# Linear attention beside a gated FFN on one core: exp and phi over two banks, rstd for two tiles, K's banks in turns, and the query projection of twelve tiles moved in front of gate/up

## The chip, the core and the metric

The kernel runs on one core of one Trainium2 chip. The metric is the device time of the whole program in microseconds. The kernel before takes 510.51 us (median of 4 runs, 510.33 to 510.68).

The core has five engines that run side by side, each with its own queue that is worked strictly in order: PE (TensorE, matrix products), DVE (VectorE), ACT (ScalarE), POOL (GpSimd) and SP (SyncE, which here only issues transfers). They wait for each other through semaphores. PE writes its results into PSUM, eight banks of 512 fp32 values in each of 128 partitions; DVE and ACT read them from there.

## The reference

The input x has 2048 tokens of width 576. It is normalised once, and two branches are added to it: a linear attention with 32 heads of width 18, and a gated FFN of width 4608.

```
xn   = (x - mean) / sqrt(var + 1e-5)
q, k, v = xn @ wqkv                       # 32 heads of 18
phi(t)  = where(t > 0, t + 1, exp(t)) + 1e-6
kv   = sum over tokens of phi(k) v^T      # per head, 18 x 18
z    = sum over tokens of phi(k)
o    = phi(q) kv / (phi(q) z + 1e-6)
out  = x + o @ wo + (gelu(xn @ w_gate) * (xn @ w_up)) @ w_down
```

All tensors are bf16; sums are taken in fp32.

## The kernel before, in words

The 2048 tokens are 16 tiles of 128. The program has a head and then four chunks of four tiles each.

**The head** works tile by tile. For tile n: `ln_half` (two statistics over column halves of 288, DVE), `ln_aggr` (DVE), `ln_rstd` (two ACT instructions, a logarithm and an exponential), the normalisation `xn` (on DVE for even tiles, on ACT for odd tiles from 3 on, the latter after a small POOL instruction `ln_bias`), and its transpose `xnT`, for tiles 0 and 1 on PE with copies by ACT and DVE, from tile 2 on by a DMA that SP issues. Then PE projects K (and for some tiles Q): `kq_mm`, five matmuls of 288 columns for each half of the columns, each half in a bank of its own. Q uses banks 6 and 7, K uses banks 4 and 5 (`KQ_BANK`). For each half, `kq_exp` (ACT) takes the exponential of k - 1 out of PSUM, and `kq_phi` (DVE) forms max(min(e, 1), k), again from PSUM; the constants that this leaves off are put back elsewhere. The next projection into a bank waits until `kq_phi` has read it. `g_accumulate` (PE, seven matmuls for a tile) sums xn^T phi(k) over the tiles in banks 0 to 3, so that K's values need not be kept and V is never projected: kv follows later from this sum and V's weights (`kv_part`). `z_add` (POOL) sums phi(k) over the tiles.

In what follows K5 is the ten matmuls of tile 5's K, Q2 those of tile 2's Q, G4 the seven matmuls of `g_accumulate` for tile 4, and xnT7 the DMA transpose of tile 7.

**The order in the head is written out by hand.** Every piece is a `step` with a name, and the string `HEAD` lists the names in the order in which they are issued: s statistics, a aggr, r rstd, b bias, n norm, t PE transpose, c the copy or DMA transpose, m a half of a projection (tile, 1 for K and 0 for Q, half), e exp, p phi, z, G, x the load of a tile, w some idle matmuls, B and g small POOL work. What the string leaves out is added in the order that a small planning function finds. As each engine's queue is in order, the string fixes each queue. The seconds written in the `step` calls serve the planner alone.

**Q of the other tiles** is projected later. `LATE` names them: 5, 6, 7, 9, 10, 11, 12, 13, 14, 15. `late_q` runs them at the start of the chunk that holds the tile. There PE works as two row tiles of 64 rows, side by side (`_Unit`): 18 matmuls of 64 rows and 288 columns for each tile, two at a time, and ACT and DVE form phi from them in `_LateQ.end`.

**After the head** the sum is copied out of PSUM (`g_copy`, `g_strip`), multiplied with V's weights and masked. Then each chunk runs late Q, 18 gate/up pairs (`gu_pair`, PE with gelu on ACT and the product on DVE, weights streamed from HBM into four rotating buffers), and the down projection of its four tiles with the attention output added (`_DownTile`). In each chunk the DVE forms the denominators of the chunk's four tiles between the gate/up pairs (`den_jobs`), from phi(q).

SP's queue issues the transfers in order: the loads of x, the DMA transposes, V's weights, the first four weight blocks of gate/up.

Of the kernel before, what the change touches and what calls it, by code (L numbers as in the profile page):

```python
# [8 lines left out]
ACT = mybir.ActivationFunctionType  # L9
ALU = mybir.AluOpType  # L10
BF16 = mybir.dt.bfloat16
F32 = mybir.dt.float32
# [3 lines left out]
P = 128  # L16
HP = 64
S = 2048
D = 576
# [3 lines left out]
NS = S // P  # L23
# [4 lines left out]
HALF = D // 2  # L28
# [14 lines left out]
Q_CUT = 3  # L43
LATE = (5,6,7,9,10,11,12,13,14,15)
PK0 = 4
# [15 lines left out]
def kernel(  # L61
# [171 lines left out]

    def ln_rstd(n):
        r = rstd[:, n:n + 1]
        nc.scalar.activation(out=r, in_=mv[:, n, 1:2], func=ACT.Ln, bias=eps_ln[:], scale=1.0)
        nc.scalar.activation(out=r, in_=r, func=ACT.Exp, scale=-0.5)

    def ln_bias(n):
        nc.gpsimd.tensor_scalar(  # L240
            out=nbias[:, n:n + 1], in0=mv[:, n, 0:1], scalar1=rstd[:, n:n + 1], scalar2=-1.0, op0=ALU.mult, op1=ALU.mult,
        )
# [36 lines left out]

    KQ_BANK = (6, 4)  # L280
    e_tiles = {}

    def kq_mm(n, which, hf):
        c = which * D + hf * HALF
        for kt in range(KT):
            nc.tensor.matmul(  # L286
                ps_all[:, KQ_BANK[which] + hf, :HALF], lhsT=xnT[:, kt, n * P:(n + 1) * P],
                rhs=wqkv_sb[:, kt, c:c + HALF], start=(kt == 0), stop=(kt == KT - 1),
            )

    def q_first(k0, k1):
        for kt in range(k0, k1):
            for hf in range(2):
                nc.tensor.matmul(  # L294
                    ps_all[:, KQ_BANK[0] + hf, :HALF], lhsT=xnT[:, kt, 0:P], rhs=wqkv_sb[:, kt, hf * HALF:(hf + 1) * HALF],
                    start=(kt == 0), stop=(kt == KT - 1),
                )

    def kq_exp(n, which, hf):
        e = e_tiles[n, which, hf] = awork.tile([P, HALF], F32, name="phi_e", tag="phi_e", bufs=8)  # L300
        nc.scalar.activation(  # L301
            out=e[:], in_=ps_all[:, KQ_BANK[which] + hf, :HALF], func=ACT.Exp, bias=neg1[:], scale=1.0,
        )

    def kq_phi(n, which, hf):
        nc.vector.scalar_tensor_tensor(  # L306
            out=(pq, pk)[which][:, n, PK0 * which + hf * HALF:PK0 * which + (hf + 1) * HALF], in0=e_tiles[n, which, hf][:], scalar=1.0,
            in1=ps_all[:, KQ_BANK[which] + hf, :HALF], op0=ALU.min, op1=ALU.max,
        )

# [149 lines left out]
    def step(name, *args, **kw):  # L462
        steps[name] = _Step(*args, **kw)
# [7 lines left out]
    W_AT = {1: 5.60, 0: (7.65, 8.45)}  # L471

    for n in range(8, NS):
        step(("x", n), "SP", 0.58, n / 2 - 2, [], lambda n=n: load_x(n, 1), ready=9.70, tail=2.6)
    for n in range(NS):
# [5 lines left out]
        step(("aggr", n), "DVE", 0.14, n - 2.1 + lead, [("stats", n, 0), ("stats", n, 1)], lambda n=n: ln_aggr(n), tail=0.07)  # L481
        step(("rstd", n), "ACT", 0.43, n - 2.1 + lead, [("aggr", n)], lambda n=n: ln_rstd(n), tail=0.07)
        if n < TD:
            for i, (k0, k1, eng) in enumerate([(0, 3, "ACT"), (3, KT, COPY[n])]):
                b = TP_BANK[n] - i
                if NORM[n] == "A":
                    if not i:
                        step(("bias", n), "POOL", 0.20, n - 2.1 + lead, [("rstd", n)], lambda n=n: ln_bias(n))
                    step(("norm", n, i), "ACT", (0.49, 0.36)[i], n - 2.1 + lead, [("bias", n)],
                         lambda n=n, k0=k0, k1=k1: ln_norm_act(n, k0 * P, min(k1 * P, D)))  # L490
                else:
                    step(("norm", n, i), "DVE", (0.26, 0.19)[i], n - 2.1 + lead, [("rstd", n)],
                         lambda n=n, k0=k0, k1=k1: ln_norm(n, k0 * P, min(k1 * P, D)), tail=0.05)
# [5 lines left out]
        else:  # L499
            if NORM[n] == "P":  # L500
                step(("norm", n), "POOL", 2.35, n - 2.1 - GL, [("rstd", n)], lambda n=n: ln_norm_pool(n))
            elif NORM[n] == "A":
                step(("bias", n), "POOL", 0.15, n - 2.1, [("rstd", n)], lambda n=n: ln_bias(n))
                step(("norm", n), "ACT", 0.77, n - 2.1, [("bias", n)], lambda n=n: ln_norm_act(n), tail=0.09)
            else:
                quiet = [("z", m) for m in range(1, n) if Z_BEHIND[m] < n][-1:]
                step(("norm", n), "DVE", 0.36, n - 2.1, [("rstd", n)] + quiet, lambda n=n: ln_norm(n), tail=0.07)
            step(("xnT", n), "SP", 1.25, n - 1.9, [("norm", n)], lambda n=n: dma_transposes(n), tail=1.6)
            ready = [("xnT", n)]
        for which, rank in ((1, n), (0, n + 0.6))[:1 if n in LATE else 2]:  # L510
            for h in range(2):
                r = rank + h / 100
                last = [m for m in range(n) if which or m not in LATE][-1:]
                free = [("phi", m, which, h) for m in last]
                if n == which == 0:
                    k0, k1 = ((0, Q_CUT), (Q_CUT, KT))[h]
                    step(("mm", 0, 0, h), "PE", 0.246 * (k1 - k0), r, ready + [("mm", 0, 0, 0)][:h],
                         lambda k0=k0, k1=k1: q_first(k0, k1), ready=W_AT[0][h], tail=0.15)
                else:
                    step(("mm", n, which, h), "PE", 0.615, r, ready + free + [("spin",)], lambda n=n, w=which, h=h: kq_mm(n, w, h),  # L520
                         ready=W_AT[which] if which else W_AT[0][1], tail=0.15)
                step(("exp", n, which, h), "ACT", 0.46, r + 0.10, [("mm", n, which, 1 if n == which == 0 else h)],
                     lambda n=n, w=which, h=h: kq_exp(n, w, h), tail=0.03)
                step(("phi", n, which, h), "DVE", 0.37, r + 0.15, [("exp", n, which, h)],
                     lambda n=n, w=which, h=h: kq_phi(n, w, h), tail=0.08)
        if n > 0:
            idle = [("norm", Z_BEHIND[n])]
            step(("z", n), "POOL", 1.40, n + 2.0, [("phi", m, 1, h) for m in (0, n) for h in range(2)] + idle + ([("z", n - 1)] if n > 1 else []),
                 lambda n=n: z_add(n, Z_BEHIND[n]))
        clear = [] if n else [("xnT", m, i) for m in range(TD) for i in range(2)]  # L530
        step(("G", n), "PE", 0.75, n + 1.15, [("phi", n, 1, 0), ("phi", n, 1, 1)] + clear, lambda n=n: g_accumulate(n, G_A))
    step(("spin",), "PE", 0.30, -1.0, [("tp", 0, 1)], lambda: spin(5))
# [4 lines left out]
    def in_order(steps):  # L537
# [17 lines left out]
    HEAD = """  # L555
        s0.1 s0.0 a0 r0 s1.1 n0.0 n0.1 s1.0 t0.0 a1 t0.1 w c0.1 c0.0 s2.1 r1 m0.1.1 e0.1.1 s2.0 m0.1.0 n1.1 a2 n1.0
        t1.1 r2 m0.0.0 p0.1.1 t1.0 m0.0.1 n2 s3.1 e0.1.0 c1.1 c1.0 e0.0.1 m1.1.1 e0.0.0 p0.1.0 s3.0 a3 p0.0.1 s4.1
        s5.0 r3 m1.1.0 m1.0.1 p0.0.0 G0 e1.1.1 m1.0.0 s4.0 e1.1.0 b3 p1.1.0 p1.1.1 c2 x9 a4 n3 m2.1.0 x8 m2.1.1
        e1.0.1 r4 e1.0.0 s5.1 B p1.0.1 e2.1.1 a5 n4 p1.0.0 e2.1.0 G1 r5 b5 p2.1.1 s7.0 m2.0.1 c3 x10 m2.0.0 p2.1.0
        s6.1 e2.0.1 n5 p2.0.1 c4 m3.1.1 m3.1.0 s6.0 e3.1.1 s7.1 e3.1.0 m3.0.1 p3.1.1 e2.0.0 a6 p3.1.0 a7 r6 r7 s8.1  # L560
        n6 G2 m4.1.1 m4.1.0 e4.1.1 s8.0 G3 p4.1.1 b7 a8 e4.1.0 p4.1.0 c5 p2.0.0 x11 c6 z1 n7 m5.1.1 x13 s9.1 s9.0 z2
        e5.1.1 m5.1.0 p5.1.1 e5.1.0 r8 a9 m3.0.0 r9 p5.1.0 c7 e3.0.1 G4 b9 m6.1.1 s10.0 e3.0.0 s10.1 n8 e6.1.1
        p3.0.1 x12 m6.1.0 G5 s13.0 m4.0.1 p6.1.1 e6.1.0 a10 p6.1.0 c8 m7.1.1 x14 m7.1.0 s11.0 n9 p3.0.0 s11.1 r10 z3
        e7.1.1 e7.1.0 e4.0.1 s12.1 a11 m4.0.0 p7.1.0 p7.1.1 z4 G6 r11 m8.1.0 n10 c9 m8.1.1 e4.0.0 e8.1.0 G7 x15
        s12.0 e8.1.1 p4.0.1 b11 p8.1.0 p8.1.1 z5 m9.1.0 n11 a12 c10 e9.1.0 s13.1 s14.1 z6 m9.1.1 p9.1.0 e9.1.1 G8
        r12 a13 r13 p9.1.1 m10.1.0 b13 m10.1.1 s14.0 e10.1.0 n12 c11 e10.1.1 G9 a14 c12 z7 p10.1.0 p10.1.1 n13
        m11.1.0 m11.1.1 p4.0.0 m8.0.1 s15.0 m8.0.0 e11.1.0 z8 s15.1 p11.1.0 r14 m12.1.0 e11.1.1 e8.0.1 a15 p11.1.1
        m12.1.1 r15 e12.1.0 c13 b15 G11 n14 p12.1.0 z9 z10 e12.1.1 m13.1.0 p12.1.1 m13.1.1 g n15 e13.1.0 c14 p8.0.1
        p13.1.0 G10 e13.1.1 c15 p13.1.1 m14.1.0 m14.1.1 e8.0.0 z11 e14.1.0 e14.1.1 G13 z12 p14.1.0 m15.1.0 e15.1.0
        p14.1.1 p8.0.0 m15.1.1 G14 z13 z14 G12 e15.1.1  # L570
    """
# [316 lines left out]
```

## Time and profile before

The profiled execution took 510.54 us by the device's count, with a span from its first to its last instruction of 508.8 us; 1.7 us lie around the span. The granted TensorE clock was 1.00 throughout.

| stretch | us from the span's start | what PE does |
|---|---|---|
| start | 0 to 9.5 | idle matmuls, then tile 0's transposes and projections as data arrive |
| head | 9.5 to 43.9 | K, Q and G of tiles 1 to 15 |
| end of the head | 43.9 to 53.9 | the rest of G, V's weights |
| chunk 0 | 53.9 to 165 | gate/up, down |
| chunks 1 to 3 | 165 to 508.8 | late Q, gate/up, down |

| group | count | mean ns |
|---|---|---|
| K and Q projections, 128 x 288 (L286) | 210 | 286 |
| rstd, logarithm (L236) and exponential (L237), one column | 16 each | 288 and 203 |
| statistics of a half (L229) | 32 | 446 |
| norm on DVE, 576 columns (L250) | 7 | 417 |
| z_sum (L214) | 13 | 1279 |

How to read it: "busy" of PE counts each matmul from its start to a modelled end, and matmuls overlap, so a mean of 286 ns does not mean that they follow each other at 286 ns. The chain of waits shows what they take one after the other. Idle time of an engine costs nothing unless the chain runs through it.

### The profile page before, as it was taken

The numbers are of one execution on the slowest core, as the hardware profiler recorded it, in microseconds if no ns is written. First come the engines' busy times: TensorE is split into PE (matmuls) and PEld (weight loads), VectorE is DVE, ScalarE is ACT, GpSimd is POOL, SyncE is SP. The second block draws the span as 40 slices with busy tenths as digits, with TensorE's granted clock in tenths as the row PEclk, the third lists the DMA queues.
The fourth block names the chain that finished last, engine by engine and source line by source line (L and its number), as shares of the span: only waits on it lengthen the run. The fifth ranks groups of instructions, "written<-read, shape, count | busy, mean of one in ns | idle before, by whom it ended". The sixth has DMA issues, their size and how long they took to land.

```text
span 508.8 us, 10854 instructions
## 1 busy us (share of the span) xinstructions
PE 503.5 (99%) x4569; PEld 303.1 (60%) x4569; DVE 215.8 (42%) x469; ACT 143.0 (28%) x273; POOL 26.5 (5%) x40
## 2 busy tenths in 40 slices
PE   8999999999999999999999999999999999999997
PEld 6888544445877544445777444445777444445774
DVE  7984555554000655554101556544101656543101
ACT  6885333324100423323000432233000432232000
POOL 3367000000000000000000000000000000000000
PEclk9999999999999999999999999999999999999999
DMA  7557699997200465565000565576000466650000
GB/s 234 117 98 191 166 290 257 243 278 200 61 23 0 127 168 162 155 172 133 13 13 1 148 169 155 164 170 113 13 13 23 131 165 152 167 130 13 13 13 23
DMA packets 120426, 62.00 MB, mean 122 GB/s; under 512 B 25842, under 2 KB 120186, under 8 KB 120378
## 3 DMA queue, kind: packets, MB, share of 16 engines
q1 hardware_dynamic: 120234, 61.17, 47.0%
q8 instruction: 35, 0.57, 0.5%
q10 hardware_dynamic: 144, 0.15, 0.1%
q14 instruction: 13, 0.11, 0.1%
HBM read 53.60 MB, written 2.36 MB: 110 GB/s over the span
## 4 chain that ended last, share of the span: by engine, by line
PE 98%; DMA 1%; DVE 0%; ACT 0%; issue 0%
PE ps_all L355 57%; PE ps_all L803 28%; PE ps_all L286 5%; PE ps_all L325 3%; PE ps_all L808 3%; DMA x_sb<-in_A_x_dram 1%; PE ps_all L791 0%; PE ps_all L332 0%; PE ps_all L404 0%; PE ps_all L743 0%; ACT xnT L275 0%; DVE stats L229 0%; PE ps_all L294 0%; PE ps_all L271 0%; DVE xn L250 0%
## 5 line engine op out<-in xcount | busy, mean ns | idle before, releaser
L355 PE MATMUL ps_all<-xnT,wg 64*128 64x512 bf16 x1152 | 272.2, 377 | 0.0
L355 PE MATMUL ps_all<-xnT,wu 64*128 64x512 bf16 x1152 | 271.7, 377 | 0.0
L698 DVE TENSOR_TENSOR hT<-ps_all,gl 128x512 bf16<-128x512 f32 x144 | 99.6, 692 | 125.2 <-ACT gl L697 125.1
L355 PEld LDWEIGHTS <-wu 64*128 64x128 bf16 x1152 | 108.5, 94 | 67.9
L355 PEld LDWEIGHTS <-wg 64*128 64x128 bf16 x1152 | 108.5, 94 | 67.7
L803 PE MATMUL ps_all<-wd_sb,hT 128*128 128x288 bf16 (+2 forms) x1152 | 147.1, 287 | 0.0
L697 ACT ACTIVATE gl<-ps_all 128x512 f32<-128x512 f32 x144 | 86.0, 597 | 185.7 <-PE ps_all L355 185.2
L803 PEld LDWEIGHTS <-hT 128*128 128x128 bf16 x1152 | 110.8, 98 | 30.9 <-issue 1.3
L817 DVE TENSOR_TENSOR res<-ps_all,x_sb 128x288 bf16<-128x288 f32 (+2 forms) x32 | 13.8, 455 | 146.3 <-PE ps_all L808 88.1
L355 PE MATMUL ps_all<-xnT,wr 64*128 64x512 bf16 x288 | 54.8, 377 | 0.0
L717 ACT ACTIVATE gl<-ps_all 128x288 f32<-128x288 f32 x20 | 7.6, 409 | 120.2 <-PE ps_all L355 118.2
L286 PE MATMUL ps_all<-wqkv_sb,xnT 128*128 128x288 bf16 x210 | 28.2, 286 | 0.2
L355 PEld LDWEIGHTS <-wr 64*128 64x128 bf16 x288 | 14.1, 94 | 16.6
L286 PEld LDWEIGHTS <-xnT 128*128 128x128 bf16 x210 | 19.8, 98 | 5.1 <-ACT xnT L275 0.7
L301 ACT ACTIVATE phi_e<-ps_all,neg 128x288 f32<-128x288 f32 x44 | 21.0, 497 | 4.9 <-PE ps_all L286 2.2
L808 PE MATMUL ps_all<-m_sb,pqT 128*128 128x288 bf16 (+2 forms) x128 | 20.9, 286 | 0.0
L325 PE MATMUL ps_all<-hT,xn 128*128 128x288 bf16 (+4 forms) x144 | 18.4, 273 | 0.0
L214 POOL TENSOR_TENSOR z_sum<-z_sum,hT 128x576 f32<-128x576 f32 x13 | 16.6, 1279 | 1.2 <-DVE xn L250 0.5
L306 DVE SCALAR_TENSOR_TENSOR hT<-phi_e,ps_all 128x288 bf16<-128x288 f32 x32 | 14.2, 450 | 5.5 <-ACT phi_e L301 5.0
L325 PEld LDWEIGHTS <-xn 128*128 128x128 bf16 x144 | 13.8, 97 | 3.5 <-issue 0.2
L808 PEld LDWEIGHTS <-pqT 128*128 128x128 bf16 x128 | 12.4, 98 | 3.3
L229 DVE BATCH_NORM_STATS2 stats<-x_sb 128x6 f32<-128x288 bf16 x32 | 13.5, 446 | 1.4 <-DMA x_sb<-in_A_x_dram 1.3
(76 smaller groups left out, 175.5 us busy)
## 6 DMA issues: line engine op xcount, KB each, us to landing
wg<-in_B_w_gate_dram SPq DMA_DIRECT2D x72, 256.0 KB, 3.1
wu<-in_B_w_up_dram SPq DMA_DIRECT2D x72, 256.0 KB, 3.5
wd_sb<-in_B_w_down_dram SPq DMA_DIRECT2D x12, 432.0 KB, 5.5
wr<-in_B_w_gate_dram SPq DMA_DIRECT2D x72, 32.0 KB, 2.7
wr<-in_B_w_up_dram SPq DMA_DIRECT2D x72, 32.0 KB, 3.1
out_dram<-res SPq DMA_DIRECT2D x15, 144.0 KB, 3.2
x_sb<-in_A_x_dram SPq DMA_DIRECT2D x11, 144.0 KB, 4.0
wqkv_sb<-in_A_wqkv_dram SPq DMA_DIRECT2D x2, 576.0 KB, 5.8
```

What stands on the lines that cost most here:

```text
L214: z = nc.gpsimd.tensor_tensor(out=z_bf[:] if n == NS - 1 else z_sum[:], in0=pk[:, 0, PK0:PK0 + D] if n == 1 else z_sum[:], in1=pk[:, n, PK ...
L229: nc.vector.bn_stats(out=ln_raw[n][:, h, :], in_=x_sb[:, n, h * HALF:(h + 1) * HALF])
L286: nc.tensor.matmul(ps_all[:, KQ_BANK[which] + hf, :HALF], lhsT=xnT[:, kt, n * P:(n + 1) * P], rhs=wqkv_sb[:, kt, c:c + HALF], start=(kt == ...
L301: nc.scalar.activation(out=e[:], in_=ps_all[:, KQ_BANK[which] + hf, :HALF], func=ACT.Exp, bias=neg1[:], scale=1.0,)
L306: nc.vector.scalar_tensor_tensor(out=(pq, pk)[which][:, n, PK0 * which + hf * HALF:PK0 * which + (hf + 1) * HALF], in0=e_tiles[n, which, h ...
L325: nc.tensor.matmul(ps_all[:, b, col:col + w], lhsT=xn[:, n, kt * P:(kt + 1) * P], rhs=pk[:, n, PK0 + d0:PK0 + d0 + w], start=(n == 0 and c ...
L355: return nc.tensor.matmul(self.outs[i], lhsT=self.lhs(i, rows, kt), rhs=self.rhs(i, rows, kt), start=start, stop=stop, skip_group_check=True,)
L697: nc.scalar.activation(out=gl[:], in_=ps_all[:, b[0], :], func=ACT.Gelu_apprx_tanh)
L698: nc.vector.tensor_tensor(out=hT[:, GUB * k + i, :], in0=ps_all[:, b[1], :], in1=gl[:], op=ALU.mult)
L803: nc.tensor.matmul(self.acc(hf), lhsT=hT[:, f, j * P:(j + 1) * P], rhs=wd_sb[:, f, self.parts[hf]], start=(f == 0 and not paired), stop=Fa ...
L808: nc.tensor.matmul(self.acc(hf), lhsT=pqT[:, c, self.ts], rhs=m_sb[:, c, self.parts[hf]], start=False, stop=(paired and c == 3), skip_grou ...
L817: nc.vector.tensor_tensor(out=self.res[:, hs], in0=self.acc(hf), in1=x_sb[:, self.n, hs], op=ALU.add)
```

## The change

Five things change, all in the head but the last.

1. `SPLIT = 2`: for tiles 2 and up, exp and phi of a projection are one ACT and one DVE instruction over both halves (576 columns in two banks) instead of one for each half. For tiles 0 and 1 they stay split.
2. `PAIRED = 4`: for tiles 4 and up, rstd is computed for two tiles at once (two columns), after the aggr of both.
3. `kq_bank`: K of tiles 5, 7, 9, 11, 13, 15 goes to banks 6 and 7, which no Q uses any more by then; K of the even tiles and of tiles 0 to 4 stays in banks 4 and 5. A projection waits for the phi of the projection that last used its banks.
4. `LATE` gains tiles 4 and 8: twelve tiles now have their Q in front of gate/up, and the head holds Q of tiles 0 to 3 only.
5. `HEAD` is a new order.

```
-LATE = (5,6,7,9,10,11,12,13,14,15)
+SPLIT, PAIRED = 2, 4
+LATE = tuple(range(4,16))
...
-    def ln_rstd(n):
-        r = rstd[:, n:n + 1]
-        nc.scalar.activation(out=r, in_=mv[:, n, 1:2], func=ACT.Ln, bias=eps_ln[:], scale=1.0)
+    def ln_rstd(n, cnt):
+        r = rstd[:, n:n + cnt]
+        nc.scalar.activation(out=r, in_=mv[:, n:n + cnt, 1], func=ACT.Ln, bias=eps_ln[:], scale=1.0)
         nc.scalar.activation(out=r, in_=r, func=ACT.Exp, scale=-0.5)
...
-    KQ_BANK = (6, 4)
+    TURN = max(n for n in range(NS) if n not in LATE) + 1
+
+    def kq_bank(n, which):
+        return 6 if not which or n > TURN and (n - TURN) % 2 else 4
...
+    def kq_out(n, which, part):
+        b = kq_bank(n, which)
+        if part < 2:
+            return ps_all[:, b + part, :HALF]
+        return ps_all[:, b:b + 2, :HALF]
+
+    def kq_exp(n, which, part):
+        w = HALF if part < 2 else D
+        e = awork.tile([P, w], F32, name=f"phi_e{w}", tag=f"phi_e{w}", bufs=4)
+        e_tiles[n, which, part] = e[:] if part < 2 else e[:].rearrange("p (h c) -> p h c", h=2)
+        nc.scalar.activation(out=e_tiles[n, which, part], in_=kq_out(n, which, part), func=ACT.Exp, bias=neg1[:], scale=1.0)
...
+        nc.vector.scalar_tensor_tensor(
+            out=out, in0=e_tiles[n, which, part], scalar=1.0, in1=kq_out(n, which, part), op0=ALU.min, op1=ALU.max,
+        )
...
+            prior = [j for j in jobs if kq_bank(*j) == kq_bank(n, which)][-1:]
+            jobs.append((n, which))
+            free = [p for j in prior for p in phis(*j)]
...
     HEAD = """
...
+        s0.0 s0.1 a0 r0 s1.0 n0.0 n0.1 s1.1 a1 t0.0 c0.0 t0.1 r1 c0.1 w s2.1 m0.1.0 s2.0 n1.1 m0.1.1 t1.1 m0.0.0 a2
+        e0.1.0 n1.0 r2 p0.1.0 t1.0 n2 m0.0.1 c1.1 s3.1 e0.1.1 c1.0 s3.0 p0.1.1 m1.1.0 e0.0.0 c2 e0.0.1 a3 p0.0.0
+        p0.0.1 e1.1.0 r3 s5.0 m1.1.1 m1.0.0 b3 x11 e1.1.1 g p1.1.0 s4.1 G0 x9 p1.1.1 m1.0.1 s5.1 s4.0 n3 x15 a5
+        e1.0.0 m2.1.0 e1.0.1 m2.1.1 c3 x8 a4 r4 e2.1.2 p1.0.0 p1.0.1 x10 G1 b5 s6.0 n4 m2.0.0 p2.1.2 s7.1 n5 m2.0.1
+        s7.0 s6.1 a7 m3.1.0 m3.1.1 c4 e2.0.2 B G2 e3.1.2 c5 x12 p2.0.2 s9.1 a6 p3.1.2 m3.0.1 r6 m3.0.0 b7 e3.0.2
+        m4.1.1 m4.1.0 n6 s8.0 e4.1.2 s8.1 a8 G3 p3.0.2 z1 n7 s9.0 m5.1.0 c6 a9 p4.1.2 r8 s10.1 z2 m5.1.1 G4 n8 b9
+        e5.1.2 s10.0 m6.1.0 z3 p5.1.2 n9 x13 m6.1.1 s11.0 s11.1 e6.1.2 a11 G5 c7 a10 c8 z4 m7.1.1 p6.1.2 r10 m7.1.0
+        n10 e7.1.2 G6 b11 z5 s13.0 z6 s12.1 m8.1.0 c9 p7.1.2 x14 m8.1.1 G7 m9.1.1 s12.0 n11 c10 a12 s13.1 e8.1.2 a13
+        p8.1.2 r12 m9.1.0 b13 n12 s14.1 m10.1.1 e9.1.2 m10.1.0 c11 c12 G8 s14.0 z7 p9.1.2 n13 z8 s15.0 s15.1 a14
+        e10.1.2 c13 a15 m11.1.1 r14 m11.1.0 e11.1.2 b15 p10.1.2 n14 z9 n15 p11.1.2 G9 m12.1.1 m12.1.0 c14 e12.1.2
+        c15 z10 p12.1.2 z11 G10 m13.1.0 m13.1.1 e13.1.2 p13.1.2 G11 m14.1.1 m14.1.0 m15.1.1 e14.1.2 m15.1.0 G12
+        p14.1.2 e15.1.2 G14 p15.1.2 z12 G13 z13 G15
     """
```

The planning numbers in the `step` calls follow (0.76 and 0.67 for the wide exp and phi) and are left out here; they issue nothing.

## Prediction

> **What bounds the kernel now.** I read the page's busy table first, then the chain of waits in order of time, then the groups by shape for durations, then the timeline of the head for the gaps between engines.
>
> The busy table:
>
> ```profile
> PE 503.5 (99%) x4569; PEld 303.1 (60%) x4569; DVE 215.8 (42%) x469; ACT 143.0 (28%) x273; POOL 26.5 (5%) x40
> ```
>
> The chain through the head (start, length, engine, what, how many instructions):
>
> ```profile
> 8.95 0.49 ACT xnT L275
> 9.44 0.05 issue
> 9.48 2.01 PE ps_all L286 x15
> 11.50 0.75 PE ps_all L325 x7
> 12.25 1.84 PE ps_all L286 x15
> 14.08 0.75 PE ps_all L325 x7
> 14.83 3.06 PE ps_all L286 x25
> 17.89 0.75 PE ps_all L325 x7
> ...
> 42.66 1.23 PE ps_all L286 x10
> 43.89 5.72 PE ps_all L325 x49
> ```
>
> From 9.48 us to the end of the head every piece of the chain is PE and each starts where the last ends; no other engine comes in between. So PE is not only busy, it never waits: ten projection matmuls take 1.23 us (0.1225 each) and a G 0.75 us, and the head lasts as long as their sum. ACT and DVE are nearly full beside it (8.79 and 9.30 us of the 10 us from 20 to 30, by the table of windows), but nothing waits for them.
>
> The chain through gate/up of chunk 1 and chunk 3, late Q included:
>
> ```profile
> 165.12 73.24 PE ps_all L355 x702
> ...
> 391.40 74.34 PE ps_all L355 x720
> ```
>
> Chunk 1 has three late tiles, chunk 3 has four: 18 more matmuls, 1.10 us more. That is the price of one late tile on the path, with its ACT and DVE work hidden, also where four stand in a row.
>
> Durations by shape (busy, mean ns of one):
>
> ```profile
> L301 ACT ACTIVATE phi_e<-ps_all,neg 128x288 f32<-128x288 f32 x44 | 21.0, 497 | 4.9 <-PE ps_all L286 2.2 <-DVE pq L306 0.9
> L717 ACT ACTIVATE gl<-ps_all 128x288 f32<-128x288 f32 x20 | 7.6, 409 | 120.2 <-PE ps_all L355 118.2 <-DVE pq L719 1.5 <-DVE gl L718 0.4
> L245 ACT ACTIVATE xn<-x_sb,nbias,rstd 128x576 bf16<-128x576 bf16 x7 | 6.0, 857 | 0.0
> L395 DVE TENSOR_SCALAR zb<-ps_all 128x576 bf16<-128x576 f32 x1 | 0.8, 757 | 0.3 <-PE ps_all L392 0.3
> ```
>
> The end of tile 14's projection in the timeline (start, length):
>
> ```profile
> 40.52 1.39 PE L286 MATMUL ps_all<-wqkv_sb,xnT 128*128 128x288 bf16 x10
> 41.34 1.11 ACT L301 ACTIVATE phi_e<-ps_all,neg 128x288 f32<-128x288 f32 x2 [0.47 <-PE ps_all L286]
> 42.48 0.46 DVE L306 SCALAR_TENSOR_TENSOR hT<-phi_e,ps_all 128x288 bf16<-128x288 f32 x1 [0.16 <-ACT phi_e L301]
> ```
>
> Ten matmuls stream for 1.23 us but end 1.39 us after their start: 0.17 us until a result can be read. Their end at 41.91 releases the second exp at 41.95 (0.04 us), which ends at 42.45, and phi starts at 42.48 (0.03 us). The "issue" piece above gives 0.05 us from a release to PE's start.
>
> **What the Trainium skill says.** "ScalarE: Activation LUTs", section "What ACT_TABLE_LOAD costs", prices an ACTIVATE whose bias is a column at about 280 ns + 0.833 ns for each element: an estimate of 520 ns for 288, where the trace has 497, and 760 ns for 576. "Perfetto Trace Analysis", section "Optimizing Scalar/DVE Operations", warns of the reverse of this change: where ACT and DVE "are causing bubbles on other engines, breaking up instructions may allow work to be completed sooner". Here pieces are joined; the trace of before shows no bubble on PE, so the warning is about what may arise. Its section "Matmuls" advises rotating groups through different banks so that evacuation overlaps the next matmuls, which is what the turns of K's banks do; before, with one pair of banks, PE filled that time with Q and G.
>
> **The change part by part.**
>
> *Q of tiles 4 and 8 leaves the head*: 2 x 10 x 0.1225 = 2.45 us of PE off the path, with 4 exps, 4 phis. *It arrives in chunks 1 and 2*: 2 x 1.10 = 2.20 us on the path. Both chunks then have four late tiles, as chunk 3 has now, and chunk 3's gate/up is no longer than chunk 1's (74.34 - 4 x 1.10 = 73.24 - 3 x 1.10). Sum: -0.25 us. The denominators of tiles 4 and 8 are due in their own chunks, after late Q, like tile 12's now.
>
> *Joined exp and phi.* Work falls: ACT by about 0.1 us a projection and DVE by as much, 16 projections; rstd for two saves six pairs of 0.29 and 0.20 us. None of it is on the path: worth nothing by itself. What counts is the longer wait from the last K matmul until phi is readable, L = 0.17 + 0.04 + E + 0.03 + P + 0.05. E is not in the trace: between 0.497 + 288 x 0.84 = 0.74 us (0.84 ns from the two gelu/exp rows: (597 - 409)/224, with L697's 597) and 0.857, the 576-wide row with two column operands. I take 0.75, between the row's slope and the skill's 0.76. P: 0.757 from the two-bank 576-wide row; a second source shows no extra (den_t, 576 wide, 749). So L = 1.80, at most 1.91. Before, with halves, it is 0.17+0.04+0.50+0.03+0.46+0.05 = 1.25.
>
> How much PE gives: in the new order G(n) comes after K(n+1), so between K(n)'s end and G(n) lie G(n-1) and K(n+1), 0.75 + 1.23 = 1.98 us; the bank is asked for again only after that. Margin 0.18 us, 0.07 at the upper end of E, if ACT and DVE are free at that moment. ACT has 0.66 + 0.77/2 + 0.43/2 = 1.26 us of work a tile. DVE has 0.66 (phi, 0.09 of it overlapping the next) + 2 x 0.37 (statistics) + 0.12 + 0.36/2 = 1.70. Both below 1.98, and the string puts about 1.0 to 1.1 us of DVE work between two phis, which fits in 1.98 - 0.66 = 1.32.
>
> I carried the new order forward from 9.48 us with these durations, engine by engine. Times at which PE would start a piece without a wait, against the time at which it may:
>
> ```
> piece   PE there   released by               at      margin
> K1 half 2  10.09   phi K0, half 2           10.05     0.04
> K2         12.70   phi K1                   12.50     0.20
> K3         15.90   phi K2                   15.73     0.17
>                    xnT3 (issued 12.43)      15.5      0.4
> Q3         17.87   phi Q2                   17.68     0.19
> K4         19.09   phi K3                   18.93     0.16
> K5         21.07   phi Q3                   20.95     0.12
> G4         22.30   phi K4                   22.13     0.17
> K7         25.02   xnT7 (issued 22.08)      24.8      0.2
> K10        30.20   phi K8                   30.0      0.2
>                    xnT10 (issued 26.4)      29.0      1.2
> K15        39.30   phi K13                  39.1      0.2
> ```
>
> G5 to G14 repeat G4's margin. So PE should stay without gaps, by thin margins. The start is unchanged: on ACT exp of K0's half 2 moves in front of tile 1's second copy, but that copy waits for PE's transposes until 8.95 us as now, and exp, started near 8.43 us, holds ACT for 0.40 us.
>
> *Loads on SP.* x11, x9, x15 (0.57 us of issue each) now stand before xnT3, where x9 and x8 stood; xnT3's issue at 12.4 us still finds the queue free. A transpose landed 2.6 to 3.1 us after its issue, once 3.9 (tile 9's, right behind a load). One more load in flight may cost xnT3 from 0 to 0.5 us more: up to 0.1 us of wait at K3; behind x14, xnT10 at 3.9 us would cost 0.1. I put 0.1 us for all of these together. Further on SP, the last transpose is issued near 35.2 instead of 39.3 us, so V's weights and the gate/up blocks start some 4 us earlier while PE arrives 2.45 us earlier: cover grows. POOL's sum has seven z_add of 1.3 us left at 33.5 us and ends before 44; PE needs it near 51.
>
> Sum against the profiled execution: 510.54 - 0.25 + 0.1 = 510.39; that execution lies 0.03 above the median, so 510.4.
>
> **Rivals.**
>
> *A, the long wait lets PE stand (slower).* Place: K5 to G14. The loop K(n) to G(n) to K(n+2) makes two tiles take 1.98 + L where L is over 1.98: each tile then costs (L - 1.98)/2 more. If DVE is regularly inside a statistics instruction (0.41 us) when exp ends, and E is 0.857, L = 2.3: 0.16 us x 11 tiles = 1.8 us, 512.1 us. It costs from L = 1.98, and decides (over 0.2%, 1.28 us after the gain) from L = 2.21. For it: margins under 0.2 us everywhere, queues in order. Against it: the DVE work between phis fits.
>
> *B, transfers and small misses*: transposes at 3.1 to 3.9 us, a stall of 0.1 to 0.4 us at four or five pieces of the table, 0.8 us in all: 511.1, no change that can be told.
>
> *C, the head was held by ACT and DVE and shrinks by all of Q, with late Q hidden*: 510.54 - 2.45 = 508.1. The 1.10 us that chunk 3 pays for its fourth late tile speaks against it.
>
> **How the numbers follow.** About 0.2% (1.0 us) is what a measurement can tell from no change. Forecast, 510.1 to 510.8: 0.57. B, to 511.5: 0.22. A, from 511.5: 0.18. C: 0.03. Faster 0.03, same 0.79, slower 0.18. The range drops C and most of A: 510.0 to 511.7.
>
> **What would show it.** The chain of after should be PE pieces without a break from 9.5 us, with K and G in turns; projections at L286's place 190 instead of 210, the 64 x 288 late matmuls 216 instead of 180; gate/up pieces of chunks 1 and 2 as long as chunk 3's, 74.34; the start of gate/up 2.4 us earlier, at 51.5. A wide exp over 0.95 us, a DVE queue that finishes statistics after exp has ended, or pieces of ACT, DVE or DMA in the chain of the head would make the prediction wrong on A's or B's side.

## The result, and the profile after

| | before | after |
|---|---|---|
| median of the runs, us | 510.56 (59 runs, 510.21 to 510.93) | 511.31 (41 runs, 510.10 to 511.87) |
| ratio | | 1.0013, 95% interval 1.0008 to 1.0017 |
| profiled execution, span, us | 510.54, 508.8 | 511.22, 509.5 |
| PE without a break from, us | 9.48 | 9.33 |
| gate/up starts at, us | 53.94 | 52.40 |

The kernel became slower by 0.75 us in the medians, 0.13% by the ratio: small, but the median lies outside all 59 runs of the kernel before. Its runs also scatter more: 8 of the 41 lie between 510.1 and 510.9, the other 33 between 511.1 and 511.9.

The groups by shape in the head of the changed kernel (count, then busy us, mean ns of one, idle time before and its releaser):

```profile
L291 PE MATMUL ps_all<-wqkv_sb,xnT 128*128 128x288 bf16 x190 | 25.8, 286 | 1.0 <-DMA xnT<-xn 0.8
L314 ACT ACTIVATE phi_e<-ps_all,neg 128x576 f32<-128x576 f32 x16 | 11.9, 741 | 10.0 <-PE ps_all L291 9.9
L322 DVE SCALAR_TENSOR_TENSOR hT<-phi_e,ps_all 128x576 bf16<-128x576 f32 x14 | 10.5, 750 | 6.3 <-ACT phi_e L314 6.1
```

The 20 matmuls are gone (190), the wide exp takes 0.741 us and the wide phi 0.750. PE's idle time is not put down to ACT or DVE, but to a transfer. The waits of PE between 3 and 54 us (us in total, times, longest) say the same; the second line is the start-up, which the kernel before has too:

```profile
PE ps_all L291 <- DMA xnT<-xn: 0.8, 1, 0.8
PE ps_all L272 <- DVE xn L251: 0.5, 1, 0.5
```

The chain of waits of the changed kernel (start, length, what), from the head into gate/up:

```profile
9.29 0.05 issue
9.33 2.01 PE ps_all L291 x15
11.34 0.75 PE ps_all L338 x7
...
22.35 0.75 PE ps_all L338 x7
23.10 1.24 PE ps_all L291 x10
24.34 0.02 issue
24.36 0.75 ACT phi_e L314
25.11 0.02 issue
25.14 0.03 DVE hT L322
25.17 0.64 issue
25.81 0.43 DVE xn L251
26.23 0.28 DVE stats L230
26.51 4.52 DMA xnT<-xn
31.03 0.04 issue
31.08 1.40 PE ps_all L291 x10
...
52.40 70.28 PE ps_all L368 x652
...
163.58 74.34 PE ps_all L368 x720
...
277.82 74.34 PE ps_all L368 x720
```

Where before had PE alone, there is one hole. Tile 10's K product at 31.08 started 0.05 us after its transpose had landed, 4.52 us after the issue. The matmul before it began at 29.96, and matmuls follow each other by 0.12 us here, so it was due at 30.08: 1.00 us lost. Behind it PE is again without a break.

What stands ahead of the transpose in this chain is tile 6's wide exp and wide phi, and behind them in DVE's queue tile 10's norm, done at 26.23. The statistics that the view names next are not read by a transpose. SP was still issuing x14 (the second line merges xnT10 and the two transposes behind it):

```profile
25.85 0.57 SPq L97 DMA_DIRECT2D x_sb<-in_A_x_dram  x1
26.51 4.89 SPq L279 DMA_TRANSPOSE xnT<-xn  x3
```

So xnT10 was issued 0.28 us after its input was ready. With x14 moved away (below) that is 0.03.

The balance: the head takes 52.40 - 9.33 = 43.07 us instead of 44.46, 1.39 less. That is -2.45 for the twenty matmuls, +1.00 at tile 10, +0.04 at tile 3 (same reading), and 0.02 of rounding. Of the five parts of the change, the longer list of late tiles is the one that reaches beyond the head. The late tiles cost what was forecast: from 163.58 to 277.82 are 114.24 us, before 113.14, and the next chunk likewise, +2.20. With PE's run starting 0.15 us earlier: -0.15 - 1.39 + 2.20 = +0.66, and the spans differ by 0.7.

What ran on the DMA engines then, from 27 to 31 us of the changed kernel (busy tenths in 40 slices of 0.1 us, GB/s of each, and the instruction queue: packets, MB, share):

```profile
DMA  6591478855999999990000000000000799999970
GB/s 58 46 115 35 150 288 311 282 144 122 353 218 248 220 133 79 23 13 0 12 12 12 0 12 12 12 12 12 20 18 18 156 255 284 289 294 294 223 132 5
q8 instruction: 1, 0.02, 1.4%
```

A packet of 16,384 bytes of instructions starts at 28.03 and ends at 28.95. From 28.6 to 30.1 the queues move some 12 GB/s, then 290. Over the whole span 36 such packets came for PE's 9,170 instructions, 64 bytes each if they are PE's, and I take them as such; a block comes every 107 to 142 matmuls in this trace.

The packets between the block's end and the recovery (window 28.90 to 30.13):

```profile
DMA packets 33, 0.02 MB, mean 12 GB/s; under 512 B 25, under 2 KB 33, under 8 KB 33
```

In the trace's own list they ran one after another: first eight rows of 1,152 bytes, to 29.80, which is a sixteenth of x14's 128 rows, then almost nothing but packets of a transpose, 256 bytes each. Such a packet usually takes 0.018 us. Twenty others, begun between 28.23 and 28.76, took 1.39 to 1.91 us and all ended between 30.14 and 30.18. I read this as the one DMA engine that had carried the block working off its share, while the transpose's packets on the other engines were held until it had caught up; the record does not name engines.

### The profile page after: what moved, and what is told of

Same layout as the page of the kernel before. It is cut to its first block, busy times and chain, and to the rows that moved or that the text cites. A ratio compares the mean times of both kernels' runs of the same rounds, so it can differ in the third digit from the quotient of the medians.

```text
span 509.5 us, 10873 instructions
## 1 busy us (share of the span) xinstructions
PE 503.9 (99%) x4585; PEld 302.7 (59%) x4585; DVE 215.8 (42%) x457; ACT 137.6 (27%) x245; POOL 26.6 (5%) x40
## 4 chain that ended last, share of the span: by engine, by line
PE 97%; DMA 1%; DVE 0%; ACT 0%; issue 0%
PE ps_all L368 58%; PE ps_all L824 28%; PE ps_all L291 4%; PE ps_all L829 3%; PE ps_all L338 3%; DMA xnT<-xn 1%; DMA x_sb<-in_A_x_dram 0%; PE ps_all L812 0%; PE ps_all L345 0%; PE ps_all L417 0%; DVE stats L230 0%; PE ps_all L764 0%; ACT xnT L276 0%; DVE xn L251 0%; ACT phi_e L314 0%
## 5 line engine op out<-in xcount | busy, mean ns | idle before, releaser
L738 ACT ACTIVATE gl<-ps_all 128x288 f32<-128x288 f32 x24 | 9.2, 410 | 121.4 <-PE ps_all L368 118.5
L291 PE MATMUL ps_all<-wqkv_sb,xnT 128*128 128x288 bf16 x190 | 25.8, 286 | 1.0 <-DMA xnT<-xn 0.8
L291 PEld LDWEIGHTS <-xnT 128*128 128x128 bf16 x190 | 17.8, 98 | 5.9 <-DMA xnT<-xn 1.3
L314 ACT ACTIVATE phi_e<-ps_all,neg 128x576 f32<-128x576 f32 (+1 forms) x24 | 15.7, 660 | 10.4 <-PE ps_all L291 10.3
L322 DVE SCALAR_TENSOR_TENSOR hT<-phi_e,ps_all 128x576 bf16<-128x576 f32 (+1 forms) x18 | 12.3, 682 | 6.3 <-ACT phi_e L314 6.1
```

Source lines behind the costliest of these rows:

```text
L291: nc.tensor.matmul(ps_all[:, kq_bank(n, which) + hf, :HALF], lhsT=xnT[:, kt, n * P:(n + 1) * P], rhs=wqkv_sb[:, kt, c:c + HALF], start=(kt ...
L314: nc.scalar.activation(out=e_tiles[n, which, part], in_=kq_out(n, which, part), func=ACT.Exp, bias=neg1[:], scale=1.0)
L322: nc.vector.scalar_tensor_tensor(out=out, in0=e_tiles[n, which, part], scalar=1.0, in1=kq_out(n, which, part), op0=ALU.min, op1=ALU.max,)
```

## The experiments

Every run was compared with the kernel before on the same chip. Its medians there were 510.46 to 510.72, so between runs on different chips the ratio says more than the median.

**The two loads.** x14 directly behind x13 instead of ahead of xnT10:

```
-... n9 x13 m6.1.1 s11.0 ...          ... p7.1.2 x14 m8.1.1 ...
+... n9 x13 x14 m6.1.1 s11.0 ...      ... p7.1.2 m8.1.1 ...
```

> The changed kernel with the load of tile 14 issued right behind that of tile 13 instead of right ahead of tile 10's transpose. Theory 'load ahead': the load just ahead on the queue is what makes xnT10 land 4.52 us after its issue; with it gone xnT10 lands in 2.6 to 3.2 us, PE no longer waits at K10 (0.83 us), time 511.3 - 0.85 = 510.4 us. Rival 'something at that moment' (PE's own instruction fetch runs over the DMA engines at 28.0 us): xnT10 is late whatever stands ahead of it, and the time stays near 511.2. Rival 'wide exp and phi': K10 waits on, the DMA only being the last of several, time stays near 511.2.

Measured: 510.52 us (510.40 to 510.90, 13 runs), 1.0002 (0.9994 to 1.0010). xnT10 still took 3.99 us, and tile 10's K product lost 0.22 us instead of 1.00. So the load in front is part of the wait, 0.78 us of it, not all. It cost in two ways: without it xnT10 was issued 3.82 us before its product was due instead of 3.57, and landed 0.53 us sooner after its issue.

x15 behind x12 instead of ahead of xnT3:

```
-... s4.0 n3 x15 a5      ... c5 x12 p2.0.2 ...
+... s4.0 n3 a5          ... c5 x12 x15 p2.0.2 ...
```

> The changed kernel with the load of tile 15 issued behind tile 12's instead of ahead of tile 3's transpose, so that two loads and not three stand ahead of xnT3. If the third load is what makes xnT3 land after 3.4 us instead of 3.1, PE's wait of 0.18 us at K3 goes and the time falls by 0.1 to 0.2 us; K10's wait stays (about 0.83 us in most executions): 511.1. If not, no difference to the changed kernel: 511.3.

Measured: 511.22 us (510.38 to 511.52, 21 runs), 1.0013 (1.0006 to 1.0019). xnT3 came 3.0 us after its issue and tile 3 lost nothing; tile 10 lost 1.12 us. In the changed kernel's profile the wait at tile 3 was worth 0.04.

Both loads moved:

> Both loads moved. If both waits are due to the loads ahead, PE has no wait in the head and the sum of the prediction without its allowance holds: 510.56 - 0.25 = 510.3 us, 0.05% under the kernel before. If the wide exp and phi cost something of their own, it stays above 510.6.

Measured: 510.50 us (510.16 to 511.26, 13 runs), 1.0002 (0.9994 to 1.0010). The profiled execution took 510.16. Its chain of waits shows the head as it was forecast:

```profile
22.98 1.23 PE ps_all L291 x10
24.20 0.75 PE ps_all L338 x7
...
28.95 2.48 PE ps_all L291 x20
31.43 0.75 PE ps_all L338 x7
...
51.09 0.26 PE ps_all L417 x5
51.35 2.69 PE ps_all L368 x23
```

PE runs from 9.26 to gate/up at 51.35, 42.09 us: 2.37 less than before. Even here xnT10 took 3.84 us and landed 0.05 before its product started.

**Parts of the change.** The kernel before with only Q of tiles 4 and 8 taken out of the head (two more entries in LATE, their twelve names out of the string):

```
-LATE = (5,6,7,9,10,11,12,13,14,15)
+LATE = tuple(range(4,16))
```

> The kernel before with Q of tiles 4 and 8 moved in front of gate/up and nothing else: halves, one pair of banks for K, the old order. If PE's stream is all that counts and halves free their bank in time (1.25 us of latency against 1.36 us between a half's end and the next matmul into its bank), it gains the 0.25 us too: 510.3 us. If the two Qs were what covered K's evacuation in one pair of banks, or DVE's work, PE waits behind the tiles that have lost them and it is over 510.6, up to 512.

Measured: 511.90 us (511.81 to 512.40, 7 runs), 1.0031 (1.0020 to 1.0043). The chain of this kernel between 20 and 27.6 us:

```profile
20.94 0.36 DVE pq L306
21.30 0.73 DVE stats L229 x2
22.03 0.35 DVE hT L306
...
27.07 0.47 DVE hT L306
27.53 0.04 issue
27.57 0.53 PE ps_all L286 x3
```

With less PE work in the head, the old order and one pair of banks for K, PE waits for DVE's phi: 0.8 us, in two waits. Taking Q out does not pay by itself. That it was the joined instructions which let Q leave is not so: in the runs below with all in halves, but the new order and the turns of banks, PE waits for no exp and no phi in the head.

Exp and phi of all tiles in halves again, the rest of the change kept (`SPLIT = 16`, eight phi_e buffers):

> The changed kernel with exp and phi split into halves again for all tiles (two instructions where it has one, eight buffers for e), everything else as changed. It puts back about 0.1 us of ACT and of DVE work for each of 16 projections and shortens the wait from the last K matmul until phi is readable from 1.77 to 1.25 us. If the wide instruction costs PE time (rival A of the prediction), this is faster than the changed kernel: 511.0 or less. If its margins hold, as the trace of the changed kernel has it, the halves bring nothing back, and DVE, with 1.8 us of work in 1.98 us a tile, may hold PE up in places: 511.2 to 512.

Measured: 510.57 us (510.22 to 511.71, 12 runs), 0.9999 (0.9991 to 1.0007). The execution that was traced took 1378.31 us, far from all others, and its trace is not read here. The same kernel a second time:

> The changed kernel with exp and phi of every tile split again into column halves, a second time for a profile that can be read. If the wide instructions delay tile 10's norm: xnT10 is issued at 26.2 or earlier and lands at least 0.4 us before 31.03, and tile 10's K product waits less than 0.4 us; median 510.4 to 510.7. If the gain of the first measurement came from where the fetch fell: xnT10 is issued at 26.4 to 26.6 as in the changed kernel, with the fetch at another place against x14, and the median can be anywhere from 510.4 to 511.3.

Measured: 510.49 us (510.21 to 511.07, 13 runs), 0.9998 (0.9989 to 1.0006). Both expectations were half met. xnT10 was issued at 26.92, but PE's work at tile 10 was 0.66 us later; the time from its issue to its due product was 3.82 us, 0.25 more than in the changed kernel. It landed after 3.44 us, 1.08 sooner, and tile 10 lost nothing. With a lead of 3.82 and a landing of 4.52 it would have lost 0.7, so in this execution the place of the block (here from 27.27) did the larger part. But the halves did something too: tile 10's norm was done 4.33 us before its product was due instead of 3.85, because tile 6's phi, ahead of it in DVE's queue, was done 0.52 us sooner after the start of K6 (2.43 us instead of 2.95). Here x14's issue, from 26.26 to 26.83, took most of that back.

All of the change, but K in one pair of banks:

```
-        return 6 if not which or n > TURN and (n - TURN) % 2 else 4
+        return 4 if which else 6
```

> The changed kernel with K in banks 4 and 5 for all tiles, no turns. With the wide exp and phi the next K waits for the phi of the tile before: 1.77 us from the last matmul, of which G covers 0.75, so from K5 to K15 each tile takes 3.0 us instead of 1.98, 11 x 1.03 = 11.3 us, less the 0.8 us of wait at K10 that this hides: about 521.7 us. If the chip does not need the turns, 511.2.

Measured: 525.25 us, a single run, about 3.5 above what was expected. PE's waits in the head of this kernel:

```profile
PE ps_all L291 <- DVE hT L322: 8.9, 8, 1.9
PE ps_all L291 <- ACT phi_e L314: 2.6, 3, 0.9
```

Wide instructions need the banks in turns: in one pair, K of the next tile stands until phi has read both banks. Its chain shows K halves starting at 23.08, 26.37 and 29.66, so a tile took 3.29 us there, where 3.0 had been expected.

**PE's instruction block.** To move it, matmuls were taken out of PE's stream ahead of the head. First, 16 fewer warm-ups (`NWARM = 19` instead of 35):

> The changed kernel with 19 idle matmuls at the start instead of 35; nothing else moves, the load of tile 14 stays ahead of xnT10. PE's instructions are fetched in blocks of 16 KB, about every 128 pairs of load and matmul; 16 pairs fewer at the start move the fetch that falls on xnT10 at 28.0 us by about 16 x 0.1225 = 2 us, to 30. Theory 'fetch': it is the fetch's 0.92 us on one DMA engine that delays xnT10's share on that engine, the load ahead only adds to it; xnT10 then lands in about 3 us, K10's wait goes, 510.3 to 510.6. Theory 'load ahead alone': nothing changes, 511.2. A cold start of PE with fewer idle matmuls would show as slower first matmuls before 9.5 us, up to 0.5 us.

Measured: 512.48 us (512.02 to 514.20, 6 runs), 1.0041 (1.0029 to 1.0052). It is no clean test: the first five matmuls of K took 1.22 us, where the changed kernel ran its first ten in 1.40, PE's run began at 10.47 instead of 9.33, and tile 3 lost 0.42 us. But the landing is telling: 14 of xnT10's 16 semaphore updates came by 30.85 us, the other two at 33.05 and 33.07, after the block (30.62 to 32.28). Tile 10 lost 1.52 us. The same with both loads moved:

> Both loads moved and 19 idle matmuls: no load ahead of xnT3 and xnT10 and the fetch elsewhere. If the fetch and the loads are all that stands between the changed kernel and the sum of its matmuls, 510.2 to 510.3 in nearly all executions, 0.05% under the kernel before; if the fetch now falls on another tight transpose (xnT11), 510.5 or more.

Measured: 513.49 us (512.63 to 513.97, 5 runs), 1.0055 (1.0042 to 1.0068). A miss for the same reason: fewer warm-ups cost more at the start than they could bring.

Then with PE as busy as ever: 17 warm-ups of 256 columns and one of 128 in place of 35 of 128.

```
...
-    spin(NWARM)
+    spin(17, 2 * P)
+    spin(1)
```

> The changed kernel with its 35 warm-up matmuls of 128 columns replaced by 17 of 256 columns and one of 128: TensorE is as busy at the start, and has 17 matmuls fewer in its instruction stream ahead of the first product. Order, loads and work are untouched. If TensorE's block of instructions (in the changed kernel's trace at 28.03, in the middle of x14's load and just ahead of xnT10's transpose) is what holds x14 until 30.29 and with it xnT10 until 31.03: the block comes about 17 x 0.12 = 2.1 us later, at 30.1, x14 lands by about 28.3, xnT10 by 29.3 to 29.8, tile 10's K product waits for nothing, and the median is 510.3 to 510.7. Rival, that x14's load and the order of SP alone make xnT10 late: xnT10 lands at 30.8 to 31.1 as before and the median is 511.2 to 511.4. Third, that the fetch only moves the harm to xnT11: xnT10 in time, xnT11 late by some 0.5 us, median 510.8 to 511.2.

Measured: 511.31 us (510.83 to 511.87, 13 runs), 1.0014 (1.0006 to 1.0022): the third case. The block came at 29.01, half the shift I had counted on. xnT10 took 2.80 us and tile 10 lost nothing; xnT11 took 4.92, and tile 11 lost 0.70; tile 3, near the head's first block, had lost 0.22. Here the chain misleads:

```profile
29.09 1.24 PE ps_all L292 x10
30.32 0.02 issue
30.35 0.75 ACT phi_e L315
31.10 0.02 issue
31.12 0.76 DVE hT L323
31.88 0.73 DVE stats L231 x2
32.61 0.26 DVE mv L234 x2
32.86 0.03 issue
32.89 1.15 PE ps_all L292 x8
```

It names statistics, which no projection reads; phi, which frees the bank, was done at 31.88. xnT11's last semaphore update came at 32.84, 0.05 before the product, the same lag as at tile 10 above. A releaser named by the view has to be one that the instruction needs.

Eight fewer (8 of 256 columns, 19 of 128):

> As the run with 17 fewer, but only 8 fewer warm-up matmuls (8 of 256 columns and 19 of 128). If the fetch is the cause: the block comes about 1.0 us later than in the changed kernel, at 29.0, when x14 is nearly through and xnT10's own packets are under way. x14 lands by about 28.4, xnT10 keeps a late remainder on the engines that carry the block, landing at 30.0 to 31.0: the wait of tile 10's K product shrinks but need not go, and the median is 510.5 to 511.3. Rival, that the fetch plays no part: x14 lands at about 30.3, xnT10 at 31.0, median 511.2 to 511.4.

Measured: 511.59 us (510.95 to 512.78, 12 runs), 1.0019 (1.0011 to 1.0028). The block hardly moved (28.15), x14 landed at 30.41, xnT10 at 31.14, tile 10 lost 1.13. The expected shift of 1.0 us was wrong, and this run can't separate the cases.

Both loads moved and 17 fewer:

> The two loads moved as before (x14 behind x13, x15 behind x12) and the warm-up with 17 matmuls fewer. If loads ahead of a transpose and the fetch are all that the change lost: no DMA piece in the head's chain of waits, and the median is 510.0 to 510.3, the sum that was forecast without its losses. If the scatter of these kernels comes from elsewhere: 510.4 to 510.6, as with the loads moved alone.

Measured: 511.37 us (510.33 to 512.14, 21 runs), 1.0014 (1.0007 to 1.0021), above both cases. Block at 29.33; xnT11 took 4.77 and tile 11 lost 0.55. With the loads out of the way the loss is back, one tile later. The traced execution took 510.92, below the median, so most executions lost more than it shows.

29 fewer (8 of 512 columns, one of 384; then 512 and 128):

> The changed kernel with 29 matmuls fewer in the warm-ups at the same columns (8 of 512, one of 384, and in the five behind tile 0's transposes one of 512 and one of 128). 17 fewer had moved TensorE's block by 1.0 us, from 28.03 to 29.01, and moved the wait from xnT10 to xnT11 (landing 4.92 us after its issue). If the block's place is what decides: it comes at 29.6 to 30.8, xnT10 (issued 26.5) and xnT11 (27.9) land within 2.6 to 3.2 us and nobody waits for them, xnT12 (issued 30.2) takes up to 4.8 us, lands by 35.0, and its K product, due at 34.2 to 34.9 then, waits at most 0.6 us; median 510.4 to 511.0. If losses of this size come without the fetch: 511.2 to 511.5, with a K product waiting for a transpose that no block crosses.

Measured: 511.75 us (511.13 to 514.86, 9 runs), 1.0037 (1.0022 to 1.0052). The block again came no later than 29.23; xnT11 took 5.01 and tile 11 lost 0.79. The place behind both transposes was not reached, so the case in which nobody is hit was not seen.

Both loads moved and all in halves:

> The changed kernel with both loads moved (x14 behind x13, x15 behind x12) and exp and phi of every tile split again into column halves; what is left of the change is that Q of tiles 4 and 8 runs ahead of gate/up, K's banks in turns, and rstd for two tiles at once. If the two cures add up: each alone brought back 0.7 to 0.8 us, which is all that was above the kernel before, and together they leave the 0.25 us that the sum of the work had promised: 510.1 to 510.4. If both cure the same wait, that of tile 10's K product on xnT10: 510.4 to 510.7, the same as each alone. If split halves make ACT and DVE late (0.99 + 0.81 us a tile against a piece of 1.98 us): over 510.8.

Measured: 510.36 us (510.21 to 511.08, 13 runs), 0.9996 (0.9988 to 1.0004): the lowest median and ratio of all, and not to be told from the kernel before. xnT10 met the block here too and took 4.27 us, but it had been issued 4.61 us before its product was due. The chain shows that thin margins remain, here tile 7's, which lost 0.23 us:

```profile
21.75 3.45 DMA xnT<-xn
25.20 0.04 issue
25.25 1.40 PE ps_all L291 x10
26.65 0.75 PE ps_all L338 x7
```

**All together.** From the traces' records, one execution each, in us from the start. A landing is the last of a transfer's 16 semaphore updates; "due" is the start of the matmul before, plus 0.12:

```
kernel           block          transpose hit        due    lost
before           26.42-27.93    xnT9   25.88-29.76   30.25  0
after            28.03-28.95    xnT10  26.51-31.03   30.08  1.00
x15 late         28.35-29.28    xnT10  26.68-31.34   30.26  1.12
8 fewer          28.15-29.09    xnT10  26.47-31.14   30.05  1.13
x14 early        27.93-28.89    xnT10  26.54-30.53   30.36  0.22
both loads       27.36-28.24    xnT10  26.14-29.98   30.01  0.02
loads + halves   27.48-28.43    xnT10  25.82-30.09   30.43  0
halves           27.27-28.55    xnT10  26.92-30.36   30.74  0
16 fewer         30.62-32.28    xnT10  28.02-33.07   31.59  1.52
both + 16        30.77-32.23    xnT11  29.66-34.43   33.92  0.55
17 fewer         29.01-30.61    xnT11  27.92-32.84   32.19  0.70
both + 17        29.33-30.54    xnT11  27.94-32.71   32.20  0.55
29 fewer         29.23-30.73    xnT11  28.18-33.19   32.45  0.79
```

In each, the transpose named here took 3.4 to 5.1 us. Two traces are not in the table: with Q alone xnT9 met the block and took 3.74 us, and with one pair of banks xnT10 met it and took 3.29; PE waited for neither. A transpose directly behind the one that was hit took up to 5.0, all others of these traces 2.5 to 3.5, so the two ranges touch. The first block of the head, at 11.4 to 15.6 us, did less (2.8 to 3.9 on xnT3 or xnT4), but in four of these traces (16 fewer, both + 16, 17 fewer, halves) tile 3 lost 0.2 to 0.5 us. With 35 warm-ups and no load in front, xnT10 landed 2.6 us after the block's start; with x14 still under way, 3.0 to 3.1. The kernel before has the block too, but it fell on xnT9, issued 4.37 us before its product was due.

The held packets are in all fifteen traces: behind the block of the table's column, 17 to 21 packets of a transpose were let go within 0.05 us of each other, 0.76 to 1.19 us after the block's end. The longest of these delays, 1.00 to 1.19, are the six traces in which eight to ten rows of a load ran in between; the other nine have none and 0.76 to 0.87. From 8 to 42 us no transpose's packet took over 0.75 us that did not end within 2.0 us after a block of this size. Blocks of 8,192 bytes on a second instruction queue (q14) lie in the head as well; what they cost was not worked out.

## Why the prediction was wrong

- *Q leaves the head, -2.45 us.* Right: 2.37 in the profile with both loads moved, with some 0.04 lost at tiles 7 and 10.
- *Late Q, +2.20.* Right, to the hundredth: 74.34 in chunks 1 and 2, and 2 x 1.10 in the starts. Rival C is out.
- *The wait L and the turns of banks.* Right: E 0.741 against 0.75, P 0.750 against 0.757, and no wait of PE for exp or phi. The thin margins held, which refutes rival A at the place that it named, K5 to G14. With one pair of banks such waits did come: 525.25. What this part left out is that tile 10's norm stands behind tile 6's phi in DVE's queue. The longer wait does not reach PE directly, but the norm is done 0.48 us later against its product (3.85 us ahead of it, with halves 4.33), and that comes off the lead of xnT10.
- *The start unchanged.* 0.15 us earlier in this execution; between 9.26 and 9.78 in others with the same warm-ups, so not laid to the change.
- *xnT3, up to 0.1 us at K3.* It landed at 15.73 instead of 15.5, and cost 0.04.
- *The step that failed*: "xnT10 (issued 26.4) 29.0 1.2" and "behind x14, xnT10 at 3.9 us would cost 0.1. I put 0.1 us for all of these together". The issue was nearly right (26.51) and so was the place; the transfer took 4.52 us, and the product was due 3.57 us after the issue instead of 3.80. That cost 1.00 us. With 1.04 instead of 0.1 the sum gives 511.3. This is near rival B's total, by one wait rather than several.

Why I took 3.9 for the upper end: the longest transpose in the trace of before, tile 9's, stood "right behind a load", and I read the load as its whole cause. (Tile 8's had taken 3.2, outside the 2.6 to 3.1 that I gave for the rest.) The block had crossed that same transfer, and two of x14's 16 updates came only at 29.10 and 29.20, the rest by 27.59. So 3.9 was no bound for a load in front; it was one draw of a load and a block. The run with x14 early separates them: without the load 3.99, with both 4.52.

"DMA: Bandwidth & Descriptors" of the Trainium skill, section "Queues, rings and completion order", says that each DMA engine takes turns between its queue rows by the packet, and that a semaphore increment lands only after every earlier write from that engine, across its queues. The order in the packets' record agrees with the first: x14's eight rows follow the block's end at 28.95 one by one. For the second, two updates of xnT10 came late with 16 fewer warm-ups, 0.77 and 0.79 us after the block's end. One block on one engine would account for one of them, so this agrees only in part. Why the packets of a transpose should wait for each other like this, no run shows.

What is shown, what is argued, and what stays open: that tile 10's wait for its transpose makes the loss is shown by the balance and by the runs with moved loads. That the block is a cause is shown by the held packets behind it in fifteen traces, and by the three runs with 17 or 29 warm-ups fewer, in which it came 1.0 to 1.3 us later and the delay went from tile 10 to tile 11; it was never removed, and that it is PE's rests on the count of bytes. The wide instructions have a part through the norm: with halves the loss is gone as well (510.57 and 510.49), but how much of that is the lead and how much the place of the block is not separated. That the scatter of the runs (8 of 41 near the kernel before) comes from where the block falls fits its jitter, 27.3 to 28.4 among the runs with 35 warm-ups, but is only argued. That the last 0.25 us can be had is open: no version beats the kernel before by more than its interval.

## What to carry to other kernels

When PE has no gap left, the next limit is the lead of each transfer, the time from its issue to the instruction that needs it. Compare that lead with the longest landing in the trace and not with the usual one, and ask of each long landing what else was on the DMA engines. A transfer that is late and harmless in one schedule is late at another place in the next: here the lead of the transpose that was hit fell from 4.37 to 3.57 us, and a delay that nobody had waited for became 1.00 us. Loads that are needed late belong ahead of the row of transposes, not between them: a load in front also holds the issuing queue, here for 0.57 us. And an engine for which nobody waits can still cost time, when a longer instruction on it puts off what a transfer has to wait for.

## What the runs showed of the hardware

- A block of 16,384 bytes of instructions, every 101 to 159 matmuls over all traces, took 0.88 to 1.65 us in the head (to 43 us), and the transposes it hit from 26 us on took 3.3 to 5.1 us, against 2.5 to 3.5 for those that were neither hit nor directly behind one that was.
- Behind such a block 17 to 21 packets of a transpose were held, and all went on within 0.05 us of each other: 0.76 to 0.87 us after the block's end, or 1.00 to 1.19 where eight to ten rows of a load ran first.
- Removing 8, 17 or 29 matmuls ahead of it moved the block by 0.1, 1.0 and 1.2 us, not by 0.12 us each; with none removed it moved by up to 1.1 us from run to run.
- Sixteen warm-up matmuls fewer cost about 1.2 us in the median (512.48 against 511.31), 1.14 of it before PE's run began in the traced executions. The same columns in fewer, wider matmuls kept the start as it was: with 17 fewer PE's run began at 9.22, against 9.33.
